# Reordering ScalarE and VectorE work and transform pieces in a one-core training step

## The chip, the cores and the metric

The kernel runs on one core of a Trainium2 chip, as one program. The metric is the device time of one execution in microseconds, given as the median of several runs. The profiled execution is a run of its own with its own time; times inside it are counted from the start of its span.

Five engines matter. TensorE (PE) multiplies from SBUF into PSUM. ScalarE (ACT) and VectorE (DVE) read PSUM, copy and compute. GpSimd (POOL) and SyncE (SP) mostly issue DMAs here. Each engine works through its own instructions in the order in which the program wrote them, and waits on semaphores for what it needs from others.

## The reference

The forward part is a gated mix of two branches of x (2048 rows of 576). The reference returns it and the gradients of all inputs of both branches:

```python
g = sigmoid((x * gate_w).sum(-1))
a = irfft2(rfft2(x) * (w_r + 1j * w_i))              # spectral branch
b = (gelu(x @ w_gate) * (x @ w_up)) @ w_down         # feed-forward branch, 4608 wide
out = g * a + (1 - g) * b
out, vjp = jax.vjp(f, x, w_r, w_i, w_gate, w_up, w_down, gate_w); vjp(grad_out)
```

So the kernel needs the forward products, their backward products, a 2-D transform of x and of the incoming gradient, and two inverse transforms.

## The kernel before, in words

**Two phases.** The first, up to about 961 us of the profile, goes over 18 groups `g` of 256 columns of the wide weights, and in each group over four row blocks `m` of 512 rows. One such pair is a step; its number is `pr = 4 * g + m`, from 0. The second phase reloads what the first stored, and forms the output and the gradient of x.

**A step.** TensorE forms `z` (gradient times `w_down`, L424 and L429), then `xy`, the gate and up products, in two halves `xy_full(0)` and `xy_full(1)` of eight 512-column products (L433, L440). ScalarE scales `z` into `da` (L452) and evacuates each half of `xy` with three instructions: `xb` (L461), `hu` (L462) and the square `q` (L459). VectorE then does `H_ew1` (L467 to L471, four instructions), ScalarE a sigmoid of `s` (L487, later L490 and L491), and VectorE `H_ew2` (L496 to L508, seven or eight). `H_ew2` of a step is queued after the jobs of that step (`sigs()`), or, in group 0, one step later (`held`). So a step starts on TensorE while VectorE still works on the step before.

**The jobs of a step.** After `xy`, a list of weight-gradient pieces follows: products `wps` with `dH` and `xn` (L570, 512 columns), with `A` and `dB` (L552, 288 columns), and a tail (L584). A finished `wps` tile is evacuated by `wcopy`, ScalarE in general, VectorE for the rest of step 6 (L521). The products with `dB` need all of `dB` scaled by `1 - g`, which `scale_dB(k, engine)` does in four parts of four instructions (L1000 on ScalarE, L1002 on VectorE).

**The transform pieces.** The spectral branch is cut into small units that stand in one list `fft`; `fft_next()` runs the next. A step gets `n` units. They are spread over the jobs by accumulated weight: unit `k` goes ahead of the first job at which `at >= total * k / n - 0.45`. In later steps one unit (`k0`) stands in `xy_full(1)`, ahead of its last four products. A forward unit is L613 with copy `Y` (L618), or L630 with copy `ve` (L633). An inverse unit is `z(p)` (L858, copy `ZT` of 128x1024, L861), `ztail(p)` (L870, copy `ZU`, L873) or `d(i)` (L884 and L886, copy `ev` of 128x580, L890). Between forward and inverse stand the table units: `tail_table` (L647 to L650) and `turned(h)` (L669 and L672, copies `RT`, L675, and `BT`, L673).

**One buffer.** All unit products and `z` of the steps share one PSUM tile (`pz`, `bufs=1`). So a unit, or the next step's `z`, can't start before the copy out of the tile before it is done. The `xy` tiles have two buffers (`ph`), the `wps` tiles two (`pw`). From group 1 on, `q` has one SBUF buffer, so the new `q` waits for the last reader of the old one in `H_ew2` (L504).

**What sets the order.** A manual schedule is on: the order of each engine is the order in which the code calls it. In step 6 `makeB` makes a small table on VectorE (L232 to L238) and `run_late` runs the sines of the tables on ScalarE (L177, L245).

Of the kernel before, what the change touches and what calls it, by code (L numbers as in the profile page):

```python
# [10 lines left out]
ALU = mybir.AluOpType  # L11
# [244 lines left out]
def kernel(  # L256
# [198 lines left out]
    def H_act(k, xy, tiles, part):  # L455
        xb, q, hu = tiles
        h = slice(2 * k, 2 * k + 2)
        if part == 0:
            nc.scalar.activation(q[:, h, :], xy[:, :, 0:FG], ACT.Square)  # L459
        else:  # L460
            nc.scalar.copy(xb[:, h, :], xy[:, :, 0:FG])  # L461
            nc.scalar.copy(hu[:, h, :], xy[:, :, FG:2 * FG])  # L462
# [178 lines left out]
    def tail_table():  # L641

        n = HF - P
        nc.gpsimd.memset(tb.At2[:], 0.0)
        tp_ = pz.tile([P, 2, 1024], BF16, tag="z", name="tp")
        for c in range(2):
            nc.tensor.transpose(tp_[:, c, 0:P], tb.Dt[2][:, c, 0:P], ident[:])  # L647
            nc.tensor.transpose(tp_[0:n, c, 256:256 + P], tb.Dt[2][:, c, P:HF], ident[:])
            nc.tensor.transpose(tp_[:, c, 512:512 + 32], tb.Dt[3][0:32, c, 0:P], ident[0:32, 0:32])
            nc.tensor.transpose(tp_[0:n, c, 768:768 + 32], tb.Dt[3][0:32, c, P:HF], ident[0:32, 0:32])  # L650
        nc.scalar.copy(tb.Oi[:, :, 0:P], tp_[:, :, 0:P])
        nc.scalar.copy(tb.Oi[:, :, P:HF], tp_[:, :, 512:512 + n])
        ot = unit([2, HF], name="ot")
        nc.scalar.copy(ot[0:n, :, 0:P], tp_[0:n, :, 256:256 + P])
        nc.scalar.copy(ot[0:n, :, P:HF], tp_[0:n, :, 768:768 + n])
        for c in range(2):
            for e, sb in enumerate((tb.Dt[1], ot)):
                r0 = 2 * n * c + (e ^ c)
                LD.dma_start(tb.At2[r0:r0 + 2 * n - 1:2, c, e, :], sb[0:n, c, :])
# [3 lines left out]
    def turned(h):  # L663

        def f():
            tp_ = pftile(BF16)
            ts = range(8 * h, 8 * h + 8)
            for k, t in enumerate(ts):
                nc.tensor.transpose(tp_[:, 0, k * P:(k + 1) * P], tb.Rt[t], ident[:])  # L669
            if h == 0:  # L670
                for v in range(2):
                    nc.tensor.transpose(tp_[:, 1, v * P:(v + 1) * P], tb.B[:, v, :], ident[:])  # L672
                nc.scalar.copy(tb.BT[:].rearrange("p v m -> p (v m)"), tp_[:, 1, 0:2 * P])  # L673
            o = unit([8, P], name="RT")
            nc.scalar.copy(o[:].rearrange("p t m -> p (t m)"), tp_[:, 0, :])  # L675
            tb.RT.extend(o[:, k, :] for k in range(8))
        return f

# [156 lines left out]
    def inv_units(s, dv, scale):  # L835
        vp, zt = {}, {}

        def pre(i0):
            def f():
                Vp = vp[i0] = unit([2, 4 * HF], name="Vp")  # L840
                v = s[:].rearrange("g (k t c) l -> (g k) t c l", k=4, c=2)[:, i0:i0 + 2]
                LD.dma_start(Vp[:, :, 0:2 * HF], v[:, :, 0])
                LD.dma_start(Vp[:, :, 2 * HF + NL:], v[:, :, 1, 0:2 * P])
                LD.dma_start(Vp[:, :, 2 * HF:2 * HF + NL], v[:, :, 1, 2 * P:])
            f.noslot = True
            return f

        tails = {}

        def z(p):  # L850

            def f():
                Vp = vp[2 * p]
                zps = pftile()
                for ii in range(2):
                    for n in range(4):
                        c0 = (2 * HF + NL) * (n // 2) + n % 2
                        nc.tensor.matmul(zps[:, ii, n * P:(n + 1) * P], lhsT=Vp[:, ii, c0:c0 + 2 * P - 1:2],  # L858
                                         rhs=tb.RT[2 * p + ii], start=True, stop=True)
                zt[p] = unit([2, 4, P], name="ZT")  # L860
                nc.scalar.copy(zt[p][:].rearrange("p i a m -> p i (a m)"), zps[:])  # L861
            return f

        def ztail(p):

            def f():
                zps = pftile()
                Vp = vp.pop(2 * p)
                for ii in range(2):
                    nc.tensor.matmul(zps[0:2 * NL, 0, ii * P:(ii + 1) * P], lhsT=Vp[:, ii, 2 * P:2 * P + 2 * NL],  # L870
                                     rhs=tb.RT[2 * p + ii], start=True, stop=True)
                tails[p] = unit([2, P], name="ZU")
                nc.scalar.copy(tails[p][0:2 * NL].rearrange("p a m -> p (a m)"), zps[0:2 * NL, 0, 0:256])  # L873
            return f

        def d(i):
            def f():
                ii = i % 2
                Z, U = zt[i // 2], tails[i // 2]
                yps = pftile()  # L880
                w = 2 * HF
                for c in range(2):
                    for e, tab in enumerate((tb.Dt[0], tb.Oi)):
                        nc.tensor.matmul(yps[:, c, e * HF:(e + 1) * HF], lhsT=Z[:, ii, 2 * c + (e ^ c), :], rhs=tab[:, c, :],  # L884
                                         start=(e == 0), stop=False)
                    nc.tensor.matmul(yps[:, c, :w], lhsT=U[0:2 * NL, ii, :], rhs=tb.At2[0:2 * NL, c].rearrange("p e l -> p (e l)"),  # L886
                                     start=False, stop=True)
                ev = unit([2, 2, HF], F32, name="ev")
                yo = unit([D + 1], name="yo")
                nc.scalar.activation(ev[:].rearrange("p c e u -> p c (e u)"), yps[:, :, :w], ACT.Copy, scale=scale)  # L890
                V.tensor_tensor(yo[:, 0:w].rearrange("p (u e) -> p e u", e=2), ev[:, 0], ev[:, 1], op=ALU.add)
                V.tensor_tensor(yo[:, D:DF - 1:-1].rearrange("p (u e) -> p e u", e=2), ev[:, 0, :, 0:HF - 1], ev[:, 1, :, 0:HF - 1],
                                op=ALU.subtract)
                LD.dma_start(dv[:, i, :], yo[:, 0:D])
            return f
        out = [z(0), ztail(0)]
        for p in range(1, T // 2):
            if p + 1 < T // 2:
                out.append(pre(2 * p + 2))
            out += [z(p), d(2 * p - 2), ztail(p), d(2 * p - 1)]  # L900
        return out + [d(T - 2), d(T - 1)], [pre(0), pre(2)]

    VC, AC = V.tensor_copy, nc.scalar.copy

    warm = pftile()
    for _ in range(30):
# [42 lines left out]
    def fft_next():  # L949
        while fft_pos[0] < len(fft):  # L950
            u = fft[fft_pos[0]]
            fft_pos[0] += 1
            u()
            if not getattr(u, "noslot", False):
                return

    def ready():
        u = fft[fft_pos[0]]
# [45 lines left out]
    for g in range(NG):  # L1004
# [3 lines left out]
        for m in range(NPR):  # L1008
# [15 lines left out]
            if g == 0:  # L1024
# [18 lines left out]
                xy = xy_full(0)  # L1043
                for f in mid_:
                    f()
                if held:
                    held.pop()()
                for part in (1, 0):
                    H_act(0, xy, tiles, part)

                def between():
                    for f in late_:
# [19 lines left out]
            else:  # L1072
# [2 lines left out]
                for f in inside:  # L1075
                    f()
                if pr == 5:
                    scale_dB(2, AC)
                xy = xy_full(0)
                if held:  # L1080
                    scale_dB(0, AC)
                    held.pop()()
                for part in (1, 0):
                    H_act(0, xy, tiles, part)
                k0 = int(n > 0 and pr > 7 and ready())
                xy = xy_full(1, fft_next if k0 else None)
                for part in range(2):
                    H_act(1, xy, tiles, part)
                if pr == 5:
                    scale_dB(3, VC)  # L1090
                state += [*H_ew1(g, tiles, da), da]
                if pr == 4:
                    scale_dB(1, VC)
                elif pr == 5:
                    build_R(nc, tb, unit, 8)
                    build_R(nc, tb, unit, 12)
                elif pr == 6:
                    next(makeB)
                side_work(4.4)
                jobs = carry + hs  # L1100
                total = sum(w for w, _ in jobs)
                at, k = 0.0, k0
                tables = {6: 0}.get(pr)
                for i, (w, f) in enumerate(jobs):
                    if k < n and (at >= total * k / n - 0.45 or len(jobs) - i <= n - k):
                        fft_next()
                        k += 1
                    if i == tables:
                        run_late(tb)
                        wcopy[0] = VC  # L1110
                    if pr == NG * NPR - 1 and at == 0.0:
                        sigs()
                    f()
                    at += w
# [259 lines left out]
```

## Time and profile before

| what | value |
|---|---|
| median of 5 runs | 1393.96 us (1393.48 to 1394.41) |
| profiled execution | 1394.13 us, its span 1392.2 us |
| TensorE busy | 1372.5 us |
| VectorE, ScalarE busy | 740.6 us, 710.1 us |
| granted TensorE clock | 1.00 |

The 1.9 us between the profiled execution's time and its span lie around the program's instructions. A busy share counts an instruction from its start to its end; TensorE's products overlap, and a few of their records are missing. A missing 512-column record looks like a hole of about 0.2 us, put down to "issue". So a stall of TensorE is best read from the distance between two starts less the time that the first one's columns take (a row of 512-column products advances by 0.216 us a product, one of 288 columns by 0.122 us).

### The profile page before, as it was taken

The page shows a single profiled execution, that of the slowest core. Times are in us where ns is not written, and L with a number is a line of the kernel's source. Part 1 is how long each engine was busy: PE and PEld are TensorE (multiplying, and loading weights), DVE is VectorE, ACT ScalarE, POOL GpSimd, SP SyncE. Part 2 cuts the span into 40 slices and gives each one's busy share as a digit, 9 for nine tenths or more (in the row PEclk, how much of TensorE's full clock was granted, in tenths as well). Part 3 has the DMA queues.
Part 4 walks back from the last instruction along what each step waited for, and adds up shares of the span by engine and source line. Part 5 has one row for each costly group of instructions (what it writes and reads, how often), then busy time and mean ns, then how long its engine had stood idle before and what let it go on. Part 6 is the DMA issues. An engine that isn't in the chain of part 4 may idle for free.

```text
span 1392.2 us, 25935 instructions
## 1 busy us (share of the span) xinstructions
PE 1372.5 (99%) x10186; PEld 913.8 (66%) x10272; DVE 740.6 (53%) x1407; ACT 710.1 (51%) x1311; POOL 245.4 (18%) x486
## 2 busy tenths in 40 slices
PE   9999999999999999999999999999999999999999
PEld 7556566566556556556566566556777777777777
DVE  7976656555888877885656666560001742121101
ACT  7876767777778778867767777651000000000000
POOL 3001110123335543422011101110000100000000
PEclk9999999999999999999999999999999999999999
DMA  7424444355466556555556465749999998787874
GB/s 224 124 81 125 118 125 114 96 155 150 122 159 160 157 146 160 142 145 134 141 142 166 137 161 155 169 117 276 203 191 201 223 193 170 162 159 164 157 150 89
DMA packets 510790, 214.49 MB, mean 154 GB/s; under 512 B 312554, under 2 KB 503724, under 8 KB 510668
## 3 DMA queue, kind: packets, MB, share of 16 engines
q1 hardware_dynamic: 493546, 187.44, 58.4%
q0 software_dynamic: 14912, 24.24, 6.4%
q8 instruction: 80, 1.31, 0.4%
q10 hardware_dynamic: 2210, 1.15, 0.4%
q14 instruction: 42, 0.34, 0.1%
HBM read 41.05 MB, written 93.84 MB: 97 GB/s over the span
## 4 chain that ended last, share of the span: by engine, by line
PE 93%; ACT 3%; DVE 3%; issue 1%; SPq 0%; DMA 0%; POOL 0%; DVEq 0%; POOLq 0%; ACTq 0%
PE acc L1224 30%; PE wps L570 16%; PE xy L440 16%; PE wps L552 10%; PE z L424 8%; PE wps L584 2%; PE xy L433 2%; PE pf L613 2%; PE z L429 2%; PE pf L630 1%; PE pf L884 1%; PE pf L811 1%; PE pf L722 1%; PE pf L886 1%; PE pf L858 0%
## 5 line engine op out<-in xcount | busy, mean ns | idle before, releaser
L1224 PEld LDWEIGHTS <-pin 128*128 128x128 bf16 x3456 | 338.0, 98 | 85.8 <-issue 0.5
L570 PE MATMUL wps<-dH,xn 128*128 128x512 bf16 x1135 | 269.9, 379 | 1.3 <-DVE dwd L521 0.5
L440 PE MATMUL xy<-wgu,xT 128*128 128x512 bf16 x1083 | 258.3, 379 | 8.3 <-issue 7.0
L440 PEld LDWEIGHTS <-xT 128*128 128x128 bf16 x1152 | 106.5, 98 | 133.0 <-issue 24.8
L570 PEld LDWEIGHTS <-xn 128*128 128x128 bf16 x1152 | 111.4, 98 | 118.7 <-issue 1.3
L1241 ACT COPY bo<-acc 128x288 f32<-128x288 f32 x32 | 12.8, 399 | 305.0 <-PE acc L1224 280.4
L552 PE MATMUL wps<-dB,A 128*128 128x288 bf16 x1152 | 154.2, 286 | 0.7 <-DVE dB L1002 0.6
L577 POOL DMA_DIRECT2D out_dram<-dw x134 | 73.0, 549 | 431.1 <-ACT dw L521 389.6
L1224 PE MATMUL acc<-wgT,pin 128*128 128x288 bf16 x1152 | 143.8, 286 | 0.0
L1224 PE MATMUL acc<-wuT,pin 128*128 128x288 bf16 x1152 | 143.6, 286 | 0.0
L1224 PE MATMUL acc<-wd_all,pin 128*128 128x288 bf16 x1152 | 142.6, 286 | 0.0
L424 PE MATMUL z<-wdT,dOT 128*128 128x256 bf16 x1152 | 137.7, 272 | 0.6 <-ACT ZT L861 0.2
L552 PEld LDWEIGHTS <-A 128*128 128x128 bf16 x1152 | 112.1, 98 | 34.3 <-issue 1.3
L452 ACT ACTIVATE da<-z,omg 128x256 bf16<-128x256 f32 x288 | 112.3, 472 | 32.9 <-PE z L429 32.8
L424 PEld LDWEIGHTS <-dOT 128*128 128x128 bf16 x1152 | 112.4, 98 | 22.8 <-issue 1.7
L461 ACT CAST xb<-xy 128x512 bf16<-128x512 f32 x144 | 85.3, 593 | 48.9 <-PE xy L440 48.5
L1296 DVE SCALAR_TENSOR_TENSOR f32t<-gwf,dlog,b16t 128x576 f32<-128x576 f32 x16 | 13.1, 817 | 172.7 <-DMA b16t<-dxa_scr 172.7
L459 ACT ACTIVATE q<-xy 128x512 bf16<-128x512 f32 x144 | 87.9, 615 | 6.9 <-PE xy L440 4.7
L462 ACT CAST hu<-xy 128x512 bf16<-128x512 f32 x144 | 87.5, 608 | 0.0
L498 DVE TENSOR_TENSOR xb<-xb,sg 128x1024 bf16<-128x1024 bf16 x48 | 33.2, 691 | 96.3 <-ACT sg L490 96.2
L521 ACT CAST dw<-wps 128x512 bf16<-128x512 f32 x72 | 42.3, 590 | 54.5 <-PE wps L570 52.3
L467 DVE TENSOR_SCALAR s<-q 128x1024 bf16<-128x1024 bf16 x72 | 30.6, 425 | 69.9 <-ACT q L459 69.7
(226 smaller groups left out, 1635.9 us busy)
## 6 DMA issues: line engine op xcount, KB each, us to landing
scr<-dH SPq DMA_DIRECT2D x144, 256.0 KB, 3.4
scr<-A SPq DMA_DIRECT2D x72, 256.0 KB, 2.5
out_dram<-dw POOLq DMA_DIRECT2D x134, 64.0 KB, 2.5
wd_all<-in_B_w_down_dram SPq DMA_DIRECT2D x3, 1728.0 KB, 9.8
out_dram<-dwd POOLq DMA_DIRECT2D x34, 144.0 KB, 2.9
scr_p<-Vt SPq DMA_DIRECT2D x32, 145.0 KB, 2.8
wgu<-in_B_w_gate_dram SPq DMA_DIRECT2D x18, 256.0 KB, 4.3
wgu<-in_B_w_up_dram SPq DMA_DIRECT2D x18, 256.0 KB, 3.3
```

What stands on the lines that cost most here:

```text
L424: nc.tensor.matmul(zo(t), lhsT=dOT[:, ci, t, :], rhs=wdT[:, ci, :], start=(t % 4 < 2 and ci == 0), stop=False)
L440: nc.tensor.matmul(xy[k][:, t % 2, :], lhsT=xT[:, ci, t, :], rhs=wgu[:, ci, :], start=False, stop=(ci == 3))
L452: nc.scalar.activation(da[:, t, :], z[:, t % 2, t // 2, :], ACT.Copy, scale=omg32[:, 4 * m + t:4 * m + t + 1])
L459: nc.scalar.activation(q[:, h, :], xy[:, :, 0:FG], ACT.Square)
L461: nc.scalar.copy(xb[:, h, :], xy[:, :, 0:FG])
L462: nc.scalar.copy(hu[:, h, :], xy[:, :, FG:2 * FG])
L498: V.tensor_tensor(xb[:], xb[:], s[:], op=ALU.mult)
L521: wcopy[0](out, in_)
L552: nc.tensor.matmul(wps[:, :288], lhsT=tl(0, t)[:, fch * P:(fch + 1) * P], rhs=dB[:, t, h * 288:(h + 1) * 288], start=(t == 0), stop=(t == ...
L570: nc.tensor.matmul(wps[:].rearrange("p a b -> p (a b)"), lhsT=xn[:, t, c * P:(c + 1) * P], rhs=kt[t // 4][1][:, t % 4].rearrange("p k f -> ...
L577: wst[0].dma_start(ov[:, c, fsl], dw[:, k, :])
L1224: nc.tensor.matmul(acc[:, :288], lhsT=src[:, r, :], rhs=w_of(r)[:, h * 288:(h + 1) * 288], start=(first and r == 0), stop=(last and r == F ...
```

## The change

The change does the following.

- `tail_table`: the same eight small transposes in another order, equal shapes next to each other.
- `turned(0)`: the `RT` copy is queued ahead of the transposes of `tb.B`, and the `BT` copy is VectorE's.
- Copies of inverse units go through `pcopy`; it is VectorE while `xy_full(1)` is written out, ScalarE elsewhere.
- Step 3: the held sigmoid and `H_ew2` of step 2 are queued after the evacuation of the first half of `xy`, not before it.
- Part 2 of `dB` is scaled by ScalarE at the end of step 4, and part 3 by ScalarE in step 5 (before: part 2 by ScalarE in step 5, part 3 by VectorE at its end).
- Step 6: `makeB` stands ahead of `H_ew1`; `run_late` and the switch of `wcopy` stand one job later.
- The unit inside `xy_full(1)` begins with step 7 (before: step 8).
- After a unit with `wide` (a `z(p)`) the next unit waits until 1.7 us of job weight have passed.

```diff
-        for c in range(2):
-            nc.tensor.transpose(tp_[:, c, 0:P], tb.Dt[2][:, c, 0:P], ident[:])
-            nc.tensor.transpose(tp_[0:n, c, 256:256 + P], tb.Dt[2][:, c, P:HF], ident[:])
-            nc.tensor.transpose(tp_[:, c, 512:512 + 32], tb.Dt[3][0:32, c, 0:P], ident[0:32, 0:32])
-            nc.tensor.transpose(tp_[0:n, c, 768:768 + 32], tb.Dt[3][0:32, c, P:HF], ident[0:32, 0:32])
+        for k, r in ((2, P), (3, 32)):
+            o = 512 * (k - 2)
+            for c in range(2):
+                nc.tensor.transpose(tp_[:, c, o:o + r], tb.Dt[k][0:r, c, 0:P], ident[0:r, 0:r])
+            for c in range(2):
+                nc.tensor.transpose(tp_[0:n, c, o + 256:o + 256 + r], tb.Dt[k][0:r, c, P:HF], ident[0:r, 0:r])
...
+            o = unit([8, P], name="RT")
+            nc.scalar.copy(o[:].rearrange("p t m -> p (t m)"), tp_[:, 0, :])
             if h == 0:
                 for v in range(2):
                     nc.tensor.transpose(tp_[:, 1, v * P:(v + 1) * P], tb.B[:, v, :], ident[:])
-                nc.scalar.copy(tb.BT[:].rearrange("p v m -> p (v m)"), tp_[:, 1, 0:2 * P])
-            o = unit([8, P], name="RT")
-            nc.scalar.copy(o[:].rearrange("p t m -> p (t m)"), tp_[:, 0, :])
+                V.tensor_copy(tb.BT[:].rearrange("p v m -> p (v m)"), tp_[:, 1, 0:2 * P])
...
-                nc.scalar.copy(zt[p][:].rearrange("p i a m -> p i (a m)"), zps[:])
+                pcopy[0](zt[p][:].rearrange("p i a m -> p i (a m)"), zps[:])
+            f.wide = True
...
+                if pcopy[0] == AC:
+                    nc.scalar.activation(evo, yps[:, :, :w], ACT.Copy, scale=scale)
+                else:
+                    V.tensor_scalar(evo, yps[:, :, :w], scale, None, op0=ALU.mult)
...
-                if held:
+                if held and m < NPR - 1:
                     held.pop()()
                 for part in (1, 0):
                     H_act(0, xy, tiles, part)
+                if held:
+                    held.pop()()
...
                 if pr == 5:
-                    scale_dB(2, AC)
+                    scale_dB(3, AC)
...
-                k0 = int(n > 0 and pr > 7 and ready())
+                k0 = int(n > 0 and pr > 6 and ready())
+                pcopy[0] = VC
                 xy = xy_full(1, fft_next if k0 else None)
+                pcopy[0] = AC
                 for part in range(2):
                     H_act(1, xy, tiles, part)
-                if pr == 5:
-                    scale_dB(3, VC)
+                if pr == 4:
+                    scale_dB(2, AC)
+                elif pr == 6:
+                    next(makeB)
                 state += [*H_ew1(g, tiles, da), da]
...
-                elif pr == 6:
-                    next(makeB)
...
-                tables = {6: 0}.get(pr)
+                tables = {6: 1}.get(pr)
                 for i, (w, f) in enumerate(jobs):
-                    if k < n and (at >= total * k / n - 0.45 or len(jobs) - i <= n - k):
+                    if k < n and (at >= max(total * k / n - 0.45, free) or len(jobs) - i <= n - k):
+                        free = at + (1.7 if wide() else 0.0)
                         fft_next()
                         k += 1
```

More of the change, by code (lines that the diff above doesn't have):

```diff
@@ L872, in f @@
                 tails[p] = unit([2, P], name="ZU")
-                nc.scalar.copy(tails[p][0:2 * NL].rearrange("p a m -> p (a m)"), zps[0:2 * NL, 0, 0:256])
+                pcopy[0](tails[p][0:2 * NL].rearrange("p a m -> p (a m)"), zps[0:2 * NL, 0, 0:256])
             return f
@@ L889, in f @@
                 yo = unit([D + 1], name="yo")
-                nc.scalar.activation(ev[:].rearrange("p c e u -> p c (e u)"), yps[:, :, :w], ACT.Copy, scale=scale)
+                evo = ev[:].rearrange("p c e u -> p c (e u)")
+                if pcopy[0] == AC:
+                    nc.scalar.activation(evo, yps[:, :, :w], ACT.Copy, scale=scale)
+                else:
+                    V.tensor_scalar(evo, yps[:, :, :w], scale, None, op0=ALU.mult)
                 V.tensor_tensor(yo[:, 0:w].rearrange("p (u e) -> p e u", e=2), ev[:, 0], ev[:, 1], op=ALU.add)
@@ L903 @@
     VC, AC = V.tensor_copy, nc.scalar.copy
+    pcopy = [AC]
     warm = pftile()
@@ L955, in fft_next, with wide @@
                 return
+    def wide():
+        return hasattr(next(u for u in fft[fft_pos[0]:] if not getattr(u, "noslot", False)), "wide")
     def ready():
@@ L1101 @@
                 total = sum(w for w, _ in jobs)
-                at, k = 0.0, k0
-                tables = {6: 0}.get(pr)
+                at, k, free = 0.0, k0, 0.0
+                tables = {6: 1}.get(pr)
                 for i, (w, f) in enumerate(jobs):
-                    if k < n and (at >= total * k / n - 0.45 or len(jobs) - i <= n - k):
+                    if k < n and (at >= max(total * k / n - 0.45, free) or len(jobs) - i <= n - k):
+                        free = at + (1.7 if wide() else 0.0)
                         fft_next()
```

## The prediction

> **What bounds the kernel now.** I read the page first, then TensorE's waits, then the timeline around each wait.
>
> ```profile
> PE 1372.5 (99%) x10186; PEld 913.8 (66%) x10272; DVE 740.6 (53%) x1407; ACT 710.1 (51%) x1311; POOL 245.4 (18%) x486
> DVE  7976656555888877885656666560001742121101
> PE z L424 <- ACT ZT L861: 0.2, 1, 0.2
> PE pf L884 <- ACT ZT L861: 0.6, 2, 0.4
> PE pf L630 <- ACT Y L618: 0.7, 1, 0.7
> PE xy L433 <- ACT hu L462: 0.6, 1, 0.6
> PE wps L552 <- DVE dB L1002: 0.6, 1, 0.6
> PE pf L669 <- ACT RT L675: 0.5, 1, 0.5
> PE wps L570 <- DVE dwd L521: 0.5, 1, 0.5
> ```
>
> TensorE is busy 99% at full clock, so no work is to be had back but its holes: 1392.2 - 1372.5 = 19.7 us, of which 7.0 are "issue" before L440, mostly missing records. No row of the second phase is among the waits, so what is saved in the first reaches the end. The rows understate: measured start to start, less the streaming time of the columns, the stalls near the edits are
>
> - steps 3 to 8: 0.78 at 46.2 (`hu`), 1.25 at 65.2 (`dB`), 0.64 at 81.3 (`dwd`), 0.85 at 91.6 (`Y`), 0.39 at 104.8 (`ve`): 3.9 us
> - tables: 0.68 (`RT`), and 1.08 for eight small transposes
> - inverse pieces: 0.40 at 683.3, 0.29 at 697.0, 0.56 at 711.7, 0.13 at 715.0, 0.35 at 779.7, then 0.40, 0.29 and 0.29 for `z` behind a `ZT` at a step's end: 2.7 us
>
> ```profile
> 47.42 2.83 ACT L1000 ACTIVATE dB<-dB,omg 128x576 bf16<-128x576 bf16 x4
> 64.77 1.20 DVE L1002 TENSOR_SCALAR dB<-dB,omg 128x576 bf16<-128x576 bf16 x4
> 76.87 0.43 DVE L467 TENSOR_SCALAR s<-q 128x1024 bf16<-128x1024 bf16 x1 [1.40 <-ACT q L459]
> 80.83 0.81 DVE L521 CAST dwd<-wps 128x288 bf16<-128x288 f32 x2
> 81.33 1.89 PE L570 MATMUL wps<-dH,xn 128*128 128x512 bf16 x7 [0.47 <-DVE dwd L521]
> ```
>
> From 43 to 82 us VectorE is the second limit (the second slice of its row is a 9): it runs nearly back to back, with one rest of 1.40. A stall cured early there is worth only what VectorE follows.
>
> **The change, by the order of instructions.** The orders of SP and POOL don't change in a single row, so no DMA moves. TensorE's changes in five places. `tables = 1` changes no engine's order: nothing of another engine stands between. VectorE gets 15 copies of inverse pieces (5 `ZT`, 10 `ev`) and `BT`, and loses four `dB` rows; ScalarE the reverse.
>
> *Steps 3 to 6.* In step 3 ScalarE was idle 1.21 until 42.17, waiting for `s`. Now it starts `xb`, `hu`, `q` when the first half of `xy` is done, 41.6, and the sigmoid at 43.0. The last `hu` ends some 0.6 earlier, so 0.6 of the 0.78 goes. But the sigmoid ends at 44.1, not 43.2, and `H_ew2`, behind which all of VectorE queues, starts 0.85 later; 0.2 of it is absorbed where L498 waited for the sigmoid at 51.2, so VectorE is 0.7 late through step 4. `dB` part 2 (2.65 on ScalarE) now runs 54.7 to 57.4, where ScalarE had rested 3.55; free. In step 5 part 3 takes its place on ScalarE, 0.7 late: 61.7 to 64.4. TensorE wants its last tile about 64.2, so about 0.3 of the 1.25 stays. VectorE saves four L1002, 1.12, but its `H_ew1` now waits for ScalarE's `q` until 66.5 (65.89 before): VectorE stays 0.6 late. TensorE, 1.5 early, enters step 6.
> There `H_ew2` of step 5 ends at 76.1. `makeB` (78.94 to 80.83, 1.9) now fills what had been the rest of 1.40, then `H_ew1` 2.05: the `dwd` copy starts near 80.0 instead of 80.83. TensorE wants the tile at 79.2 and starts at 80.5 instead of 81.33. So of the 1.5 only 0.8 is left: the `dwd` stall grows to 1.3. Bounds: nothing, if ScalarE is a little later with `dB`; 2.0, if VectorE follows as TensorE does. I take 0.8.
>
> *Step 7.* The unit L613 moves four products earlier; between it and L630 stand 4 + 4 products, 1.7 us, not 0.86. `Y` (0.65) fits in between the two `q`. But `ve` now queues behind `q`, `xb`, `hu`, as in step 8, where this cost 0.39. Gain 0.85 - 0.42 = 0.43. (Bounds 0.2 and 0.85.)
>
> *Tables.* Steps between unequal transposes take 0.11 to 0.17, equal ones follow after 0.05 or less by their columns. Four unequal steps instead of eight: 1.08 becomes 0.7, gain 0.35 (bounds 0 and 0.5). `RT` can start at the end of the eighth transpose, 303.4, not 303.76, and ends 304.4; VectorE, idle at that time, copies `BT` beside it. TensorE starts `turned(1)` at 304.46, not 304.83: 0.37.
>
> *More products after a z piece.* Three `d` units move one job later:
>
> ```profile
> 709.82 0.61 PE L858 MATMUL pf<-RT,Vp 128*128 128x128 bf16 x8
> 710.60 1.04 ACT L861 CAST ZT<-pf 128x1024 bf16<-128x1024 f32 x1
> 711.69 0.22 PE L884 MATMUL pf<-Dt,ZT 128*128 128x145 bf16 x1 [0.39 <-ACT ZT L861]
> ```
>
> `ZT` takes 1.02 to 1.04, four products cover 0.86 (eight of 288 columns 0.98), twice as many 1.73 or 1.96. The stalls 0.40, 0.29, 0.56 go: 1.25. What is late next is the `ztail` after `d`, with `ev` (0.65) to be hidden by 0.86 to 0.98: the slack of 0.87 to 1.11 that these places show shrinks to 0.01 to 0.13, so I charge 0.1 in sum. The `z` of the next step behind a `ZT` is not a unit; the stalls 0.40, 0.29, 0.29 stay.
>
> *Copies on VectorE.* VectorE's queue makes each wait for L508, the last of `H_ew2`, and holds the `H_ew1` behind it.
>
> ```profile
> L890 ACT ACTIVATE ev<-pf 128x580 f32<-128x580 f32 x32 | 21.4, 667 | 14.7 <-PE pf L886 14.6
> L861 ACT CAST ZT<-pf 128x1024 bf16<-128x1024 f32 x16 | 16.4, 1022 | 4.7 <-PE pf L858 4.6
> L521 DVE CAST dwd<-wps 128x288 bf16<-128x288 f32 x2 | 0.8, 447 | 0.0
> ```
>
> (Groups by shape, the first two from 640 to 860 us.) The last row is the nearest one: an fp32 PSUM tile copied by VectorE. [...] The gain is ScalarE's: at 778.9 an `ev` waited 0.26 behind `q`, `xb`, `hu` that a `ZT` had pushed back, and this stalled L870 by 0.35; 0.3 of it goes.
>
> **Sum**: 0.8 + 0.43 + 0.35 + 0.37 + 1.25 - 0.1 + 0.3 = 3.4 us. Against the profiled execution (span 1392.2, 1.9 around it, 1394.13) this gives 1390.7; the median of the runs is 0.17 lower: 1390.6.
>
> **The rivals.**
> *VectorE follows (in "faster").* If the sigmoid's delay is absorbed early, the cures of steps 3 to 6 come in full: 2.7 - 0.8 more or so, 5.3 in all: 1388.7. For it: VectorE loses 1.12 of `dB`. Against it: no rest in its row from 51 to 75.
> *The first part gives nothing.* `dB` part 3 stands on ScalarE ahead of `xb`, `hu`, `q`, whose lateness stops VectorE; if it costs 0.8 more than I set, steps 3 to 6 end even: 2.6 left, 1391.4, and 1392.1 if the tables fail too; both within 0.2%. For it: the slack at 64 us is nil already.
> [...]
> *It doesn't do what it says.* True of the table index alone; all else shows in the orders.
>
> **How the numbers follow.** The sum as worked out, 1389.4 to 1391.1: 0.47. VectorE follows: 0.15. So faster 0.62. First part nothing, to about 1396: 0.31. Slower 0.07. The likeliest is 1390.6. The range 1388.0 to 1394.2 takes in the bounds (all at their best 2.6 more gain, the "nothing" case with 2 us to spare) and leaves out the slower case and some 0.1 of tails.
>
> **What would show it.** Right: TensorE's wait for `hu` nearly gone, that for `dB` under 0.4, that for `dwd` up to 1 us or more, `ve` instead of `Y` in step 7; L884 with no wait for `ZT`; `RT` about 0.3; VectorE's `ev` rows near 0.75 and `ZT` near 1.2. Wrong: TensorE waiting for a VectorE `ev` or `ZT`; the `dwd` wait not above 0.7; new waits for `ev` before L870 over 0.1 each.

## The result and the profile after

The changed kernel takes 1391.16 us (median of 24 runs, 1390.70 to 1391.78) where the kernel before takes 1394.16 (42 runs). The ratio is 0.9978, 95% interval 0.9973 to 0.9984. That is 3.0 us; the prediction had 3.4 and a time of 1390.6.

The span of the profiled execution is 1389.7 us. The first line is the page's busy times, the others are TensorE's waits (engine and line, what it waited for, us in total, times, longest), as they answer to those of before:

```profile
PE 1370.4 (99%) x10187; PEld 912.9 (66%) x10272; DVE 752.7 (54%) x1419; ACT 702.3 (51%) x1299; POOL 245.2 (18%) x486
PE pf L675 <- ACT RT L672: 1.1, 1, 1.1
PE wps L570 <- DVE dwd L521: 1.1, 1, 1.1
PE pf L613 <- ACT ve L633: 0.4, 2, 0.2
PE z L424 <- ACT ZT L862: 0.2, 1, 0.2
```

The rows of `hu`, `dB`, `Y` and of `ZT` before L884 are gone. The row of `dwd` has doubled, as forecast. By starts, 0.2 of the `hu` stall and 0.3 of the `dB` stall are left, in gaps too small for a row. The row of `RT` has doubled too, and that was not forecast: 0.5 before, 1.1 now.

The clearest account comes from the starts of the 72 steps (the first L424 of each), set against those of before. They are counted here from the start of step 3, because that start itself differs by up to 2.4 us between the fourteen profiled executions (36.50 us in `copies_twice`, 38.88 in `held_undone`): TensorE's wait for the load at L395, for one, is 0.8 us in the changed kernel's profile, 1.1 in that of `held_undone` and has no row before.

| stretch | forecast | measured |
|---|---|---|
| steps 3 to 6 (start of step 7) | -0.8 | -0.88 |
| step 7 | -0.43 | -0.59 |
| `tail_table` and `turned` | -0.72 | +0.21 |
| inverse pieces | -1.45 | -1.44 |
| all, to the start of step 71 | -3.4 | -2.72 |

Minus is faster. Between these stretches the two executions keep step within 0.02 us, over hundreds of microseconds: nothing that was saved was lost again in the second phase. (The medians differ by 3.0, the profiled executions by 2.7: the changed kernel's profiled execution, 1391.42, is 0.26 above its median, and its runs lie up to 0.6 from it.)

### The profile page after: what moved, and what is told of

It reads as the page before. It is cut to its first block, busy times and chain, and to the rows that moved or that the text cites. A ratio compares the mean times of both kernels' runs of the same rounds, so it can differ in the third digit from the quotient of the medians.

```text
span 1389.7 us, 25927 instructions
## 1 busy us (share of the span) xinstructions
PE 1370.4 (99%) x10187; PEld 912.9 (66%) x10272; DVE 752.7 (54%) x1419; ACT 702.3 (51%) x1299; POOL 245.2 (18%) x486
## 4 chain that ended last, share of the span: by engine, by line
PE 94%; DVE 3%; ACT 2%; issue 1%; DMA 0%; SPq 0%; DVEq 0%; ACTq 0%
PE acc L1239 30%; PE wps L570 17%; PE xy L440 17%; PE wps L552 9%; PE z L424 8%; PE wps L584 2%; PE xy L433 2%; PE pf L613 2%; PE z L429 2%; PE pf L886 1%; PE pf L812 1%; PE pf L630 1%; PE pf L723 1%; PE pf L888 1%; PE pf L859 1%
## 5 line engine op out<-in xcount | busy, mean ns | idle before, releaser
L552 PE MATMUL wps<-dB,A 128*128 128x288 bf16 x1152 | 153.7, 286 | 0.1
L424 PE MATMUL z<-wdT,dOT 128*128 128x256 bf16 x1152 | 137.7, 273 | 0.5 <-ACT ZT L862 0.2
L552 PEld LDWEIGHTS <-A 128*128 128x128 bf16 x1152 | 112.1, 98 | 33.2 <-issue 0.3
L424 PEld LDWEIGHTS <-dOT 128*128 128x128 bf16 x1152 | 112.4, 98 | 22.5 <-issue 1.7
L498 DVE TENSOR_TENSOR xb<-xb,sg 128x1024 bf16<-128x1024 bf16 x48 | 33.2, 691 | 94.3 <-ACT sg L490 94.2
L1270 DVE SCALAR_TENSOR_TENSOR b16t<-b16t,g,f32t 128x576 bf16<-128x576 bf16 x16 | 13.1, 818 | 95.3 <-DMA b16t<-a_scr 95.0
```

What stands on the lines that cost most here:

```text
L424: nc.tensor.matmul(zo(t), lhsT=dOT[:, ci, t, :], rhs=wdT[:, ci, :], start=(t % 4 < 2 and ci == 0), stop=False)
L498: V.tensor_tensor(xb[:], xb[:], s[:], op=ALU.mult)
L552: nc.tensor.matmul(wps[:, :288], lhsT=tl(0, t)[:, fch * P:(fch + 1) * P], rhs=dB[:, t, h * 288:(h + 1) * 288], start=(t == 0), stop=(t == ...
```

## The experiments

All times below come with the kernel before run on the same chip; its medians there differ by up to 0.26 us, and a difference between two changed kernels from different chips carries that. "By step starts" is the measure just described, against before. It comes from one profiled execution of each kernel, but it repeats: the seven kernels that have the edit of the held sigmoid all gain 0.57 at the start of step 5. The times alone tell `dB_undone` and `copies_twice` from the change, since the 95% intervals of their ratios to before (0.9985 to 1.0001, 1.0011 to 1.0024) don't meet the change's. Those of `bt_second`, `late_sines`, `held_undone`, `makeB_undone` and `best` overlap with it, so what is said of these against the change rests on the traces. Theory A is the ledger of TensorE's stalls, with VectorE as the second limit from 43 to 82 us.

| run | median us | before | by step starts |
|---|---|---|---|
| the change | 1391.16 | 1394.16 | -2.72 |
| steps_alone | 1392.54 | 1394.04 | -1.45 |
| tables_alone | 1394.15 | 1394.04 | +0.22 |
| inverse_alone | 1392.55 | 1394.04 | -1.42 |
| bt_second | 1390.51 | 1394.04 | -3.54 |
| copies_alone | 1393.85 | 1393.90 | -0.23 |
| spread_alone | 1392.53 | 1393.90 | -1.26 |
| copies_twice | 1396.40 | 1393.90 | +2.54 |
| late_sines | 1390.61 | 1393.90 | -3.30 |
| held_undone | 1390.74 | 1394.09 | -3.20 |
| dB_undone | 1392.97 | 1394.09 | -1.23 |
| makeB_undone | 1391.50 | 1394.09 | -2.67 |
| best | 1389.83 | 1393.93 | -4.05 |

**The three parts one by one.** The edits are the hunks of the change, put into the kernel before: those of steps 3 to 7; those of `tail_table` and `turned`; those of `pcopy` and `wide`.

> The kernel before with the edits of steps 3 to 7 alone (held sigmoid, dB parts, makeB, the unit in step 7). Theory A (a ledger of TensorE's stalls, with VectorE as second limit from 43 to 82 us): 1.3 to 1.5 us faster than before, 1392.8, with the dwd stall at 80.6 near 1.2 as in the changed kernel. Rival B (the gain is ScalarE's lighter load in the inverse pieces): within 0.4 of before.

> The kernel before with the edits of tail_table and turned alone. Theory A: the grouped transposes give 0.35 to 0.4 back, but the transposes of tb.B now wait for the RT copy (0.68 becomes 1.27), so 0.2 us slower than before, 1394.3, no difference that the times can tell; the trace shows TensorE waiting 1.1 for RT before L670's neighbour. Rival C (that stall came only from steps shifted elsewhere): 0.7 faster, 1393.4, as the prediction had it.

> The kernel before with the VectorE copies and the wider spacing of the inverse pieces alone. Theory A: 1.4 to 1.5 us faster than before, 1392.7. Rival C (the three parts are not independent, since all hang on VectorE): under 0.8 or over 2.2.

The parts add up: -1.45 + 0.22 - 1.42 = -2.65, and together they gave -2.72. The ratios are 0.9989 (0.9983 to 0.9996) for the steps and 0.9988 (0.9982 to 0.9995) for the inverse pieces; for the tables 1.0002 (0.9994 to 1.001), so of the +0.22 only the trace speaks.

**Why the tables gave nothing.** The timeline of the kernel before in `turned(0)` and at the start of `turned(1)`, then that of the changed kernel in `turned(0)`:

```profile
303.18 0.28 PE L672 MATMUL pf<-ident,Btab 128*128 128x128 bf16 x2
304.83 0.61 PE L669 MATMUL pf<-ident,Rt 128*128 128x128 bf16 x8 [0.51 <-ACT RT L675]
```

```profile
301.65 1.01 ACT L672 COPY RT<-pf 128x1024 bf16<-128x1024 bf16 x1 [1.49 <-PE pf L670]
302.72 0.27 PE L675 MATMUL pf<-ident,Btab 128*128 128x128 bf16 x2 [1.10 <-ACT RT L672]
303.10 0.29 DVE L676 COPY BTtab<-pf 128x256 bf16<-128x256 bf16 x1 [2.12 <-PE pf L675]
```

`RT` runs from 301.65 to 302.66. The transposes of `tb.B` write the other half of the same tile, yet they start at 302.72, when `RT` is done, and TensorE stands still for the whole copy. The stall by starts is 1.27, for 0.68 before. So 0.59 is lost here, and the grouped transposes give 0.38 back (1.08 before, 0.70 now by starts; 0.35 forecast). The test takes the write behind the reader away:

```diff
-            o = unit([8, P], name="RT")
-            nc.scalar.copy(o[:].rearrange("p t m -> p (t m)"), tp_[:, 0, :])
-            if h == 0:
+            if h == 1:
                 for v in range(2):
                     nc.tensor.transpose(tp_[:, 1, v * P:(v + 1) * P], tb.B[:, v, :], ident[:])
+            o = unit([8, P], name="RT")
+            nc.scalar.copy(o[:].rearrange("p t m -> p (t m)"), tp_[:, 0, :])
+            if h == 1:
                 V.tensor_copy(tb.BT[:].rearrange("p v m -> p (v m)"), tp_[:, 1, 0:2 * P])
```

> The changed kernel with the transposes of tb.B and the BT copy moved from turned(0) to turned(1), ahead of the RT copy there. Theory A (a write into the shared PSUM tile waits for every earlier reader of the tile, wherever it reads): no wait inside turned(1); turned(0) is left with RT alone, a stall near 0.3, so 0.9 to 1.0 us faster than the changed kernel, 1390.2. Rival D (the BT copy is late because VectorE's queue is): the stall stays near 1.2 and moves, 1391.2.

```profile
301.58 1.01 ACT L675 COPY RT<-pf 128x1024 bf16<-128x1024 bf16 x1 [1.49 <-PE pf L670]
302.65 0.61 PE L670 MATMUL pf<-ident,Rt 128*128 128x128 bf16 x8 [0.24 <-ACT RT L675]
303.09 0.28 PE L673 MATMUL pf<-ident,Btab 128*128 128x128 bf16 x2
303.40 1.01 ACT L675 COPY RT<-pf 128x1024 bf16<-128x1024 bf16 x1 [0.32 <-PE pf L673]
304.45 0.29 DVE L677 COPY BTtab<-pf 128x256 bf16<-128x256 bf16 x1 [3.54 <-ACT RT L675]
```

The timeline of `bt_second`: `turned(1)` waits 0.24 (0.40 by starts), and the transposes of `tb.B` follow at once. The tables are now 0.65 faster than before by step starts, and the run 0.65 us faster than the changed kernel by its median, or 0.82 by step starts. That is less than the 0.9 to 1.0 expected; the stall behind `RT` alone was set at 0.3 and is 0.40. Rival D, a late VectorE, would have left the stall. Only the transposes of `tb.B` and the `BT` copy were moved, and the wait of 1.10 went with them: in this program the write waited for a copy out of the other half of its tile. The last two rows show that a copy did too. `BT` reads the second half only, whose transposes are done by 303.37, and VectorE is idle, yet it starts at 304.45, when ScalarE's `RT` copy of the first half has ended at 304.41. Whether the wait belongs to the tile as such, or to some other unit that holds both halves, no run separates.

**VectorE's copies and the spacing.** `copies_alone` has the hunks of `pcopy`, `spread_alone` those of `wide`.

> The kernel before with only the copies of inverse pieces in xy_full(1) moved to VectorE. Theory A: only the stall of 0.35 before L870 at 779.7 shrinks, so 0.2 us faster, 1394.0, no difference that the times can tell. Rival B (relief of ScalarE is what makes the inverse stage faster): 1.0 or more faster.

> The kernel before with only the wider spacing after a z piece. Theory A: the three stalls of L884 behind ZT go (0.40, 0.29, 0.56), so 1.2 us faster, 1392.9. Rival B: under 0.4 faster.

Nearly all of the inverse stage is the spacing: -1.26, ratio 0.999 (0.9984 to 0.9997). TensorE's timeline of the changed kernel at one of the three places has eight products behind a `z` piece where there were four, and no wait for `ZT`:

```profile
707.99 0.61 PE L859 MATMUL pf<-RT,Vp 128*128 128x128 bf16 x8
708.44 1.89 PE L570 MATMUL wps<-dH,xn 128*128 128x512 bf16 x8
710.17 0.23 PE L886 MATMUL pf<-Dt,ZT 128*128 128x145 bf16 x1
```

The copies give -0.23, 0.21 of it at the one place named; by the times, 0.9997 (0.9989 to 1.0006), they can't be told from nothing. ScalarE's relief is worth that much and no more. How near VectorE's copies come to the path is asked by doing each twice:

```diff
-                    V.tensor_scalar(evo, yps[:, :, :w], scale, None, op0=ALU.mult)
+                    for _ in range(2):
+                        V.tensor_scalar(evo, yps[:, :, :w], scale, None, op0=ALU.mult)
```

and likewise for `ZT`.

> The changed kernel with each VectorE copy of an inverse piece done twice, one after the other. Theory A (the slacks read in the trace of the changed kernel decide: a second ev takes about 0.67, a second ZT 1.13, and only what exceeds the slack less 0.05 is paid): 0.5 at the last d, 0.9 at three z, 0.6 at one, about 3.8 us slower than the changed kernel, 1395.0. Rival E (VectorE's queue carries delays on): 6 us slower or more. Rival F (the copies are off the path altogether): no change.

Groups by shape of the changed kernel (640 to 860 us), then the timeline and the waits of `copies_twice`:

```profile
L896 DVE TENSOR_SCALAR ev<-pf 128x580 f32<-128x580 f32 x10 | 7.6, 757 | 4.3 <-PE pf L888 3.9 <-DMA wdT<-wtmp 0.4
L862 DVE CAST ZT<-pf 128x1024 bf16<-128x1024 f32 x5 | 6.1, 1222 | 3.5 <-PE pf L859 3.5
```

```profile
664.62 1.56 DVE L898 TENSOR_SCALAR ev<-pf 128x580 f32<-128x580 f32 x2 [0.70 <-PE pf L889]
719.70 2.48 DVE L863 CAST ZT<-pf 128x1024 bf16<-128x1024 f32 x2
```

```profile
PE pf L887 <- DVE ZT L863: 3.2, 4, 0.9
PE pf L873 <- DVE ev L898: 0.5, 1, 0.5
```

The single copies measured 757 and 1222 ns; near 0.75 and 1.2 had been forecast. The doubled kernel is 5.24 us slower than the changed one, not 3.8. That is nearer to the 6 of rival E, but nothing is carried on: the delays arise one by one at the tile's next use, and none is added behind the last copy. The large ones are those named: four `ZT` stop TensorE by 1.03, 0.78, 1.02 and 1.02 (start to start), the last `ev` by 0.65. What was mis-sized is the second copy. It writes what the first wrote, and it did not overlap it: two `ZT` took 2.48, two `ev` 1.56, so each second one cost 1.26 and 0.80, not 1.13 and 0.67; five more places with slacks of 0.77 and 1.16 then paid 0.15 to 0.18 each. The slacks hold: single copies cost nothing, but the tightest slacks are 0.30 (three of the five `ZT`) and 0.20 (the last `ev`).

**Which edits of steps 3 to 7 carry the gain.** Three were taken back one by one in the changed kernel. First the held sigmoid, queued before the first half of `xy` again (`if held: held.pop()()` ahead of the `H_act` calls).

> The changed kernel with the held sigmoid of step 2 ahead of the first half of xy again. Theory A (VectorE limits steps 3 to 6, and this edit delays it by 0.85): the hu stall is back near 0.78 in place of 0.2, but H_ew2 runs 0.7 earlier up to step 6, and the dwd stall of 1.2 shrinks to 0.1: about 0.6 us faster than the changed kernel, 1390.5. Rival H (the edit is worth the stall that it takes away): 0.6 us slower, 1391.8.

The timeline of the changed kernel, then TensorE's waits and VectorE's timeline of `held_undone`:

```profile
43.18 1.07 ACT L487 ACTIVATE s<-s 128x1024 bf16<-128x1024 bf16 x1
44.28 0.69 DVE L498 TENSOR_TENSOR xb<-xb,s 128x1024 bf16<-128x1024 bf16 x1 [1.07 <-ACT s L487]
66.63 0.43 DVE L467 TENSOR_SCALAR s<-q 128x1024 bf16<-128x1024 bf16 x1 [0.92 <-ACT q L459]
80.08 0.82 DVE L521 CAST dwd<-wps 128x288 bf16<-128x288 f32 x2
80.59 1.89 PE L570 MATMUL wps<-dH,xn 128*128 128x512 bf16 x7 [1.05 <-DVE dwd L521]
```

```profile
PE xy L433 <- ACT hu L462: 0.6, 1, 0.6
PE pf L613 <- ACT ve L633: 0.7, 2, 0.5
```

```profile
45.07 0.69 DVE L498 TENSOR_TENSOR xb<-xb,s 128x1024 bf16<-128x1024 bf16 x1 [0.19 <-ACT s L487]
81.04 0.89 DVE L521 CAST dwd<-wps 128x288 bf16<-128x288 f32 x2
```

This execution's step 3 begins 1.69 later than that of the changed kernel. Less that, L498 starts at 43.38, not 44.28, and `dwd` at 79.35, not 80.08. The `hu` stall is back (0.77 by starts); the `dwd` stall is down from 1.22 to 0.27. The 0.3 that was left of the `dB` stall is gone as well. By step starts the kernel gains 0.73 up to step 7, keeps 0.48, and its median is 0.42 below the changed kernel's (0.35 when each is set against its own kernel before). So by the traces the edit, which does remove most of the stall at its place, costs the kernel 0.5 us. The 0.26 that `held_undone` loses again before step 8 is a longer wait for `ve` (0.65 by starts, for 0.39).

Next, the parts of `dB` as before: part 2 by ScalarE in step 5, part 3 by VectorE at its end.

> The changed kernel with dB part 2 by ScalarE in step 5 and part 3 by VectorE at its end, as before. Theory A: the dB stall of step 5 is back and larger (1.3 to 2.0 in place of 0.3), but step 6 waits for VectorE, which is only 0.1 to 0.3 later for it, so the dwd stall gives most back: 0.1 to 0.4 us slower than the changed kernel. Rival H (stalls count at face value): 1.0 to 1.7 us slower.

TensorE's waits and ScalarE's timeline of `dB_undone`:

```profile
PE wps L552 <- DVE dB L1012: 1.1, 1, 1.1
PE pf L613 <- ACT ve L633: 1.0, 2, 0.7
PE wps L552 <- ACT dB L1010: 0.4, 1, 0.4
```

```profile
78.75 1.28 ACT L177 ACT_TABLE_LOAD   x1
89.31 0.60 ACT L459 ACTIVATE q<-xy 128x512 bf16<-128x512 f32 x1 [0.89 <-DVE xb L504]
```

The expectation failed in size: 1.49 slower by step starts, 1.8 by the median, about what rival H had. The mechanism is there, since the `dwd` stall of 1.22 is gone. VectorE's L467 is 0.1 later, as expected. But the stalls before L552 sum to 2.5 by starts, not 1.3 to 2.0, so 0.96 is left at step 7. Another 0.5 comes up in step 7: TensorE reaches the unit of step 6 2.2 late, the sines behind its `Y` begin 1.7 later (table load at 78.75, where the changed kernel, shifted to the same start, has 77.01), and the sigmoid, `H_ew2`, `q` and `ve` follow. So moving `dB` is the edit that carries the steps: without it nothing is left of the 1.48 at the start of step 8.

Then `makeB`, behind `H_ew1` again.

> The changed kernel with makeB behind H_ew1 in step 6 again. Theory A: VectorE has no rest left there, so the order of the two doesn't matter: within 0.15 us of the changed kernel, the dwd stall within 0.1 of its 1.22. Rival H (this edit is what brings the dwd copy forward): 0.7 us slower or more.

VectorE's timeline of `makeB_undone`:

```profile
75.03 0.69 DVE L508 TENSOR_TENSOR dH<-dH,xb 128x1024 bf16<-128x1024 bf16 x1
75.64 0.42 DVE L467 TENSOR_SCALAR s<-q 128x1024 bf16<-128x1024 bf16 x1
79.59 0.81 DVE L521 CAST dwd<-wps 128x288 bf16<-128x288 f32 x2
```

By step starts it is -2.67 for -2.72, with a `dwd` wait of 1.1 and 1.22 by starts in both. The median is 0.34 higher than the changed kernel's, with runs from 1390.74 to 1393.40; the ratios to before, 0.9982 (0.9975 to 0.9989) and 0.9978 (0.9973 to 0.9984), don't tell the two apart. The rest of 1.40 ahead of L467 is gone here too, with `makeB` behind `H_ew1`: TensorE enters step 6 earlier by 1.46, so ScalarE has `q` ready at 75.44, before L508 ends. With VectorE busy throughout, the order of these two pieces of its work changed 0.05 by step starts. The fourth edit, the unit in step 7, was not taken back alone.

**Taking the `dwd` wait away instead.** `late_sines` is `bt_second` with `tables = {6: 2}`: ScalarE evacuates the first `dwd` ahead of the sines.

> bt_second with the sines of the tables and the switch of wcopy one job later still, so that ScalarE evacuates the first dwd of step 6 before the sines. Theory A: the dwd stall of 1.2 goes, but the sigmoid behind the sines is 0.45 later, and with it H_ew2, q and Y of step 7, where up to 0.8 comes back: 0.3 to 0.6 us faster than bt_second, 1389.8. Rival G (VectorE isn't what limits step 6): no gain.

TensorE's waits and ScalarE's timeline of `late_sines`:

```profile
PE pf L613 <- ACT ve L633: 1.0, 2, 0.7
PE pf L630 <- ACT Y L618: 0.8, 1, 0.8
```

```profile
88.43 0.60 ACT L459 ACTIVATE q<-xy 128x512 bf16<-128x512 f32 x1 [1.52 <-DVE xb L504]
88.92 0.64 ACT L618 CAST Y<-pf 128x580 bf16<-128x580 f32 x1
```

No wait for `dwd` is left, and step 7 starts 1.22 earlier than in `bt_second`. By step 8 all of it and 0.29 more is lost. The expectation had the sign wrong: it allowed 0.8 to come back, and 1.5 did. The end is the one that rival G named, no gain, but not its reason, since the 1.22 at step 7 shows that VectorE's `dwd` did limit step 6. By the trace, the one `q` buffer is what returns it: `q` waits 1.52 for the L504 of a `H_ew2` whose sigmoid stands behind the sines (no run gave `q` a second buffer).

**Both mends.** `best` is the changed kernel with the edit of `bt_second` and the held sigmoid where it was before.

> The changed kernel with both mends: the transposes of tb.B and the BT copy in turned(1), and the held sigmoid of step 2 where it was before the change. Theory A (the two lie in different stages and add): 0.65 to 0.95 from the tables and 0.45 from steps 3 to 8, so 1.1 to 1.4 us faster than the changed kernel and about 4.1 faster than before, 1390.0. Rival C (gains of one stage are lost in another): no faster than the better of the two mends alone, 1390.5.

1389.83 us, ratio 0.9971 (0.996 to 0.9981): 4.1 us faster than before and 1.3 faster than the change. The two mends add (-4.05 by step starts; -2.72 - 0.82 - 0.48 = -4.02). Its profiled execution gives 0.3 of this back once, in the second phase, where TensorE waits for a load (`pin`, at 1057.7); no other execution does so, and whether the earlier arrival is the cause is open. Of its waits, those near the edits:

```profile
PE pf L613 <- ACT ve L633: 0.7, 2, 0.5
PE xy L433 <- ACT hu L462: 0.6, 1, 0.6
PE pf L670 <- ACT RT L675: 0.2, 1, 0.2
PE z L424 <- ACT ZT L863: 0.2, 1, 0.2
```

Of the stalls listed before the change, `ve`, `hu`, a part of `RT`, and the `ZT` behind which the next step's `z` stands are left.

## Why the prediction was right, and where it was not

- *Second limit.* Right. "A stall cured early there is worth only what VectorE follows": of the 1.46 saved up to step 6, 0.88 was left at step 7, where 0.8 was forecast; `dwd` started at 80.08 (80.0 forecast) and its stall grew to 1.22 (1.3). `held_undone` shows the cause: the same stall cured costs more than it brings. It is a limit and not the whole account: `dB_undone`, expected from it at 0.1 to 0.4, came out at 1.49.
- *Parts of that sum.* The first term was seen as a gain of 0.6 whose price, 0.85 on VectorE, comes back later; that the price is the larger one by 0.5 was not drawn from it, though the numbers were there. "`makeB` now fills what had been the rest of 1.40" has the right number for the wrong reason: `makeB_undone` reaches `dwd` at the same time after step 3 begins, because the earlier TensorE takes the rest away. The edit counted for nothing, and the agreement isn't owed to it.
- *Step 7.* Right in its kind: TensorE waits 0.39 for `ve` in place of `Y`. The stretch gave 0.59 instead of 0.43; `dB_undone` shows that part of it hangs on how early step 6 is, and the edit was not tried alone.
- *Tables.* Wrong, and the step that failed is "TensorE starts `turned(1)` at 304.46, not 304.83: 0.37". It took the `RT` copy, the transposes of `tb.B` and the `BT` copy to run beside each other, as they read and write different halves of the tile. They waited for each other instead: the term was +0.59, not -0.37. The start of `RT` right behind the eighth transpose came as forecast, and the grouped transposes measured 0.38 against 0.35.
- *More products after a z piece.* Right: a gain of 1.25 was forecast, less 0.1 for the `ztail` behind `d`, and 1.26 was measured alone; the `ztail` paid next to nothing.
- *Copies on VectorE.* Right: alone they cost nothing (0.23 faster by step starts), and gave 0.2 of the 0.3 forecast at L870. No run ahead of the prediction shows a VectorE copy of these shapes: the times near 0.75 and 1.2, that the copies add nothing to the sum, and the 0.07 for a slower kernel rest on the author's estimate. In its place the changed kernel's rows show 757 ns for `ev` and 1222 for `ZT`. VectorE's copy out of PSUM is the longer one in these rows, 757 for ScalarE's 667 ns and 1222 for 1022; it decides nothing here, since slack covers it. `copies_twice` shows the point from which it would: the slack is 0.30 at the `ZT` and 0.20 at the last `ev`, and copies longer by 1.26 and 0.80 made the kernel 5.24 us slower.
- *The table index.* Right: it changed no engine's order. `tables = 2` does, as `late_sines` shows.
- *Luck in the sum.* The tables fell short by 0.93 (a gain of 0.72 forecast, a loss of 0.21 measured). The whole falls short by 0.68 only because steps 3 to 7 gave 0.24 more than forecast.

## What to carry to other kernels

Where one engine is 99% busy, as TensorE is here, count what a change is worth in that engine's stalls, measured start to start, but ask of each cure which second engine sets the next wait: what was saved ahead of the saturated VectorE came through only as far as VectorE followed (0.88 of 1.46), and a delay of VectorE cost more than the stall that it cured (by 0.5). A write into a shared tile that is queued behind a copy out of it waited for the copy in this program (1.10 in the changed kernel), even where they touch different halves, and a second engine's copy waited for the first's (`BT` in `bt_second`: 304.45, with its products done by 303.37). So queue all writes of a tile ahead of its first reader, and don't count on two engines emptying it side by side. To cover a copy of 1.02 us, put more product time behind it than the copy takes (0.86 fell short, 1.73 sufficed) before moving it to an engine where it takes 1.22.

## What the runs showed of the hardware

- On VectorE, an instruction that uses what the one ahead of it wrote did not overlap it in the rows named here. In the kernel before, L496 reads the `xb` of L498 and starts at 43.98, 0.03 us after L498 has ended (43.26 and 0.69); L497 uses nothing that L496 wrote and starts at 44.59, 0.08 before L496 has ended (43.98 and 0.69). In `copies_twice`, where the second copy writes what the first wrote, two copies took 2.48 us for twice 1.22, and 1.56 for twice 0.76.
- Among the eight small transposes of the changed kernel, a step between unequal shapes took TensorE 0.10 to 0.15 us by starts, and one between equal shapes 0.04 to 0.06. The eight went from 1.08 to 0.70.
- The start of step 3 came between 36.50 and 38.88 us in the profiled executions, a spread larger than most effects here; hence the count from step 3.
